# Four places for combined weights in a seven-product MoE stage, and two weight groups prepared later

## The chip, the cores and the metric

The kernel runs on one core of one Trainium2 chip. The metric is the device time of one launch in microseconds. Three runs of the kernel before gave 1232.5, 1235.75 and 1235.85 us; the median is 1235.75 us.

## What is computed

Three layers follow each other, all in float32, on 2304 tokens of width 512 (4 batches of 576).

```python
scores = scale * np.matmul(q, k.transpose(0, 1, 3, 2))     # 4 batches, 8 heads, 576 x 64
scores = np.where(mask, scores, -1000000000.0)             # causal by blocks of 64
attn = np.exp(scores - max) / (sum + 1e-09)
x = np.matmul(attn, v)                                     # to 2304 x 512
h = np.maximum(np.maximum(x @ w1, x @ w2), x @ w3)         # d_ff 768
x = h @ w_out
for e in range(4):                                         # second block, F 1024
    h = np.maximum(x @ w1[e], 0.0)
    out += p[:, e:e + 1] * (h @ w2[e])
```

## The kernel before, in words

Every float32 operand is split in a high and a low part, and each product is three matmuls (high by high, high by low, low by high) that accumulate in PSUM.

**Order of the work.** The attention goes through 16 pairs of heads (4 batches of 4). Batches 0 to 2 of the first MoE block (`moe1`, L543) run as filler work between the attention's steps: a generator yields after some matmuls, and `filler.upto` (L680) advances it to a count. While batch 2's filler work goes on, the last attention pairs run. Batch 2 ends with four output slices of `moe1_out` (L533), each with a `w_out` weight tile (`wo<-held`, 768 KB, two places).

**Fourth batch.** `moe1_last` (L573) computes the fourth batch's 512 tokens, with the 64 remaining tokens of all batches, as two halves of 384 by two halves of the width, in seven products instead of eight (Strassen-Winograd). A loop over j (3) and n (3) gives nine groups. A group has seven products `b11`, `t2`, `t1`, `b21`, `t3`, `b22`, `t4`, each of 6 matmuls 128x384 (`product`, L617). It takes three weight tiles: `w0`, of 512 KB, for b11 and b21; `w1`, of 256 KB, for t4; and `w2`, of 1 MB, which holds the combined weights of the four others. These were made earlier by `sums` (L515) and stored in DRAM as `summed`. The load of `w2` (L603) takes its place from the tags xh and xl by turns, which are the token tiles of batch 2. `w0` and `w1` take places of `wt` (three) and of the wide `wo` (two), five in turn (`WT`, L460 to 476). Between the products DVE and ACT add PSUM results and temporaries in the arena (`plus`, L589; the copy `q1`, L652; `close`, L623), the maxima stand in `mt` and `mr` (two of each), and at n = 2 the maximum is split into hh and hl (L646, L647).

**What runs beside the stage.** `combine` (L831) makes the seven token combinations (`put` with ACT's cast L803 and DVE's subtraction L804). `weights_in` (L947) prepares a first-layer weight group of the second block: a raw load of 512 KB (`t<-in_e_w`, L955), four sums on DVE (L926 to 929), two casts on ACT (L933), two subtractions on DVE (L935), a store of 1.8 MB (`ka<-w`, L958). A later call for the same group is a reload (`w<-ka`, L945). The program's tail advances the filler by counts between these calls: groups (0,2) and (0,3) first, with their store only, then (0,0) and (0,1), which stay in their places `w1`. Then comes the second block's first pass, with `hidden2` (seven products, L980) and `second` (L1062 to 1066).

**Queues and memory.** All these loads and stores are issued by SP's queue, in the order of the program. The pool `x2` (`xp`) is opened when the attention pool `attn` closes and lies on its memory; its tags are `w1` (two places of 1.8 MB), `t`, `pr` and the seven token tiles. Twelve small loads of `pr` (L784, L792) are kept in program order; `prs` and `prt` follow from them (L794 to 797). The order of the instructions on each engine is made by a scheduler from the program.

```python
for n in (2, 3):
    filler.upto(filler.done + 14)
    weights_in(0, n)
ready = []
for n in range(2):
    filler.upto(filler.done + 14)
    ready.append(weights_in(0, n))
```

Of the kernel before, what the change touches and what calls it, by code (L numbers as in the profile page):

```python
# [28 lines left out]
def program(tc, q, k, v, w123, w_out, probs, e_w1, e_w2, out):  # L29
# [64 lines left out]

    QT, QW = S - 64, S + 64
    pairs, later, made, exps, normal, least = {}, [], {}, [], [], []
    def rounded(engine, to, x):
# [445 lines left out]
    def moe1(b):  # L543
# [8 lines left out]
        for at, (ff, n) in enumerate(order):  # L552
# [3 lines left out]
            if n == 0:  # L556
                prev[ff] = mp.tile([P, MAIN], F32, name="mt", tag="mt", bufs=2)
                nc.scalar.copy(prev[ff], m)
            else:
                nc.vector.tensor_tensor(prev[ff], m, prev[ff], op=ALU.max)  # L560
# [9 lines left out]
            yield  # L570
        yield from moe1_out(b, [(MAIN, hh, hl, lambda d: x2f[b][:, d, 0:MAIN])])

    def moe1_last(xc):  # L573
# [19 lines left out]
        for j in range(NF // 2):  # L593
            state = {}
            for n in range(3):
                w0 = moe_weight(b, 6 * j + n, at)
                w1 = moe_weight(b, 6 * j + 3 + n, at + 1, KH)
                at += 2
                tag = ("xh", "xl")[n + j & 1]
                w2 = mp.tile([P, KD, MAIN], F32R, name=tag, tag=tag).rearrange(  # L600
                    "p d (s f) -> p (d s) f", s=2
                ).rearrange("p (x s) f -> p x s f", x=2)
                nc.sync.dma_start(  # L603
# [19 lines left out]
                def close(key, i, x=None):  # L623
                    if n == 0:
                        tag = ("mt", "mr")[key[1]]
                        t = mp.tile([P, (MAIN, CT)[key[1]]], F32, name=tag, tag=tag, bufs=2)[:, 0:CT]
                        state[key] = t
                        if x is None:
                            nc.scalar.copy(t, ms[i])
                        else:  # L630
                            plus(t, ms[i], x)
                    else:
                        t = state[key]
                        x = ms[i] if x is None else plus(x, ms[i], x)
                        nc.vector.tensor_tensor(t, x, t, op=ALU.max)
# [16 lines left out]
                nc.scalar.copy(q1, ms[0])  # L652
                yield
                product(1, "t2", True, False)
                u = plus(temp(), ms[1], q1)
                yield
                product(2, "t1", True, False)
                v = plus(temp(), ms[2], q1)
                yield
# [58 lines left out]
    for n in range(NALL):  # L718
# [13 lines left out]
        for m, st in enumerate(todo):  # L732
# [9 lines left out]
            at = (n + (m + 1) / len(todo)) / NPAIR  # L742
            filler.upto((at - 1) * UNITS - (LAG if b < B - 1 else 2 * LAG))
        if n + 4 < NALL:
# [85 lines left out]

    def combine(b11, b12, b21, b22):  # L831
        made = {}
# [13 lines left out]
        put("b11", b11, nc.vector)  # L846
        t1 = less(0, b12, b11)
        t2 = less(1, b22, t1)
        yield
        put("t2", t2, nc.vector)  # L850
        yield
        put("t1", t1, nc.vector)

# [421 lines left out]
    ends = [x for ds in (slice(0, KH), slice(KH, KD)) for x in (x2f[B - 1][:, ds, 0:CT], rest_x[:, ds])]  # L1275
    following = combine(*ends)
    xc = next(following)
    filler.work.append(moe1_last(xc))
    for _ in following:
        filler.upto(filler.done + 1)  # L1280
    for n in (2, 3):
        filler.upto(filler.done + 14)
        weights_in(0, n)
    ready = []
    for n in range(2):
        filler.upto(filler.done + 14)
        ready.append(weights_in(0, n))
    filler.upto(filler.done + 8)
    following = combine(*blocks(0))
    xc = next(following)  # L1290
    for _ in following:
        filler.upto(filler.done + 4)
    filler.rest()
# [32 lines left out]
    def temp():  # L1326
        return pe.tile([P, CT], F32, name="tmp", tag="tmp", bufs=NTMP)
# [149 lines left out]
```

## Time and profile before

| | |
|---|---|
| median of three runs | 1235.75 us |
| the profiled execution | 1238.21 us, its span 1236.4 us, mean granted clock 0.988 |
| PE busy | 1191.0 us (96%) |
| DVE, ACT, POOL busy | 903.2, 484.9, 282.9 us |
| DMA | 307.18 MB, mean 248 GB/s |
| the stage of the seven products | about 405 to 484 us |

Times are microseconds from the start of the span. In a timeline a row has the start, the duration, the engine, the line, the operation, output and inputs, the shape and the count; the brackets at the end tell how long the engine stood idle before it and what released it. PEclk is the granted TensorE clock, as a share of 2.4 GHz. Busy matmul times overlap in part, so the pitch of matmuls is read from rows with different counts. A DMA row gives the median from issue to landing.

### The profile page before, as it was taken

How to read it: one execution, taken by the hardware profiler on the slowest of the kernel's cores; microseconds unless marked ns; L12 is line 12 of the kernel's file. 1: busy time of each engine (PE TensorE's matmuls, PEld its weight loads, DVE VectorE, ACT ScalarE, POOL GpSimd, SP SyncE). 2: the span in 40 equal slices, each digit the busy share in tenths (PEclk: the TensorE clock that was granted, in tenths of full speed). 3: DMA queues.
4: the chain of work that ended last, by engine and by line, in shares of the span. 5: the costliest groups of instructions: out<-in, count | busy, mean ns of one | idle time of the engine just before them, and what ended most of it. 6: DMA issues, size and time to landing. Idle time of an engine off the chain costs nothing.

```text
span 1236.4 us, 18275 instructions
## 1 busy us (share of the span) xinstructions
PE 1191.0 (96%) x6887; PEld 1068.6 (86%) x6887; DVE 903.2 (73%) x1570; ACT 484.9 (39%) x1008; POOL 282.9 (23%) x300
## 2 busy tenths in 40 slices
PE   7889999999998998999999999999999999999998
PEld 4567777777776987989999998999999999999998
DVE  5867876544666676468878895768787888586896
ACT  6866664445335223234434441233232223322232
POOL 2558853442332000233343341000000000000000
PEclk8989999999999999999999999999999999999999
DMA  5836766744545894588888874867888887776754
GB/s 213 285 112 217 251 219 209 237 149 127 180 171 180 304 376 165 182 310 305 330 307 301 308 246 159 313 251 301 329 301 315 315 314 270 256 263 226 256 205 178
DMA packets 84939, 307.18 MB, mean 248 GB/s; under 512 B 9004, under 2 KB 20596, under 8 KB 69492
## 3 DMA queue, kind: packets, MB, share of 16 engines
q1 hardware_dynamic: 84852, 306.02, 68.9%
q8 instruction: 54, 0.88, 0.3%
q14 instruction: 33, 0.27, 0.1%
HBM read 213.42 MB, written 92.57 MB: 247 GB/s over the span
## 4 chain that ended last, share of the span: by engine, by line
PE 72%; DVE 10%; DMA 9%; ACT 5%; issue 2%; POOL 1%; SPq 0%; DVEq 0%; ACTq 0%; POOLq 0%
PE m L980 24%; PE o L1139 17%; PE m L487 13%; PE m L617 3%; PE tt L284 2%; PE pv L319 2%; PE st L186 2%; PE o L1062 2%; ACT p L230 2%; PE o L1066 2%; PE o L1065 2%; DMA summed<-arena 2%; PE m L1139 2%; DMA t<-in_e_w 2%; DMA part<-in_e_w 2%
## 5 line engine op out<-in xcount | busy, mean ns | idle before, releaser
L980 PE MATMUL m<-t,w 128*128 128x384 f32 x1152 | 228.4, 336 | 0.0
L1139 PE MATMUL o<-hx,w 128*128 128x384 f32 x1176 | 226.1, 337 | 0.6 <-DMA w<-kb 0.6
L1139 PEld LDWEIGHTS o<-hx,w 128*128 128x128 f32 x1176 | 207.9, 188 | 0.9 <-PE m L980 0.9
L980 PEld LDWEIGHTS m<-t,w 128*128 128x128 f32 x1152 | 203.6, 188 | 2.5
L980 PE MATMUL m<-b,w 128*128 128x384 f32 x864 | 175.5, 336 | 0.3 <-ACT tmp L1005 0.3
L980 PEld LDWEIGHTS m<-b,w 128*128 128x128 f32 x864 | 153.2, 188 | 3.7 <-ACT tmp L1005 0.7
L230 ACT ACTIVATE p<-st,mn 128x128 f32<-128x128 f32 (+2 forms) x144 | 78.6, 557 | 71.5 <-DVE mn L223 71.3
L256 POOL TENSOR_SCALAR p<-p,sm 128x128 f32<-128x128 f32 (+4 forms) x108 | 78.7, 743 | 105.7 <-ACT high L124 51.5
L1000 DVE TENSOR_TENSOR tmp<-m,tmp 128x384 f32<-128x384 f32 x144 | 78.1, 551 | 21.8 <-PE m L980 21.5
L935 POOL TENSOR_TENSOR w<-part,w 128x512 fp32r<-128x512 f32 x32 | 49.1, 1557 | 194.9 <-PE m L980 136.7
L487 PE MATMUL m<-xh,wt 128*128 128x512 f32 x256 | 85.7, 400 | 0.0
L223 DVE TENSOR_REDUCE mn<-st 128x1 f32<-128x128 f32 (+2 forms) x144 | 68.1, 512 | 16.5 <-ACT p L230 7.3
L1110 ACT CAST hx<-hq 128x768 fp32r<-128x768 f32 x49 | 40.6, 836 | 98.9 <-PE o L1139 75.8
L284 PE MATMUL tt<-ident,p 128*128 128x128 f32 x400 | 62.0, 286 | 16.1 <-ACT eh L294 6.6
L1062 PE MATMUL o<-w,hh 128*128 128x512 f32 x192 | 74.8, 391 | 0.9 <-ACT hh L1040 0.5
L1065 PE MATMUL o<-w,hh 128*128 128x512 f32 x192 | 74.9, 390 | 0.0
L1066 PE MATMUL o<-w,hl 128*128 128x512 f32 x192 | 74.8, 391 | 0.0
L284 PEld LDWEIGHTS tt<-ident,p 128*128 128x128 f32 x400 | 47.2, 145 | 30.5 <-ACT eh L294 8.3
L487 PE MATMUL m<-hh,wo 128*128 128x512 f32 x192 | 66.2, 411 | 6.6 <-DMA wo<-held 5.0
L935 POOL TENSOR_TENSOR part<-mix,part 128x512 fp32r<-128x512 f32 x32 | 44.8, 1414 | 70.0 <-ACT part L933 64.2
L1110 ACT CAST hx<-part 128x768 fp32r<-128x768 f32 x28 | 23.3, 836 | 91.4 <-PE o L1139 69.4
L1111 DVE TENSOR_TENSOR hx<-hq,hx 128x768 fp32r<-128x768 f32 x49 | 46.7, 955 | 16.0 <-ACT hx L1110 15.7
(221 smaller groups left out, 2265.0 us busy)
## 6 DMA issues: line engine op xcount, KB each, us to landing
w<-kb SPq DMA_DIRECT2D x55, 1024.0 KB, 5.5
w<-ka SPq DMA_DIRECT2D x30, 1792.0 KB, 7.8
ka<-w SPq DMA_DIRECT2D x16, 1792.0 KB, 6.7
kb<-part SPq DMA_DIRECT2D x16, 1024.0 KB, 7.0
wt<-held SPq DMA_DIRECT2D x28, 512.0 KB, 5.3
kb<-w SPq DMA_DIRECT2D x16, 768.0 KB, 4.9
arena<-in_w SPq DMA_DIRECT2D x18, 512.0 KB, 4.8
wo<-held SPq DMA_DIRECT2D x12, 768.0 KB, 5.0
```

The source lines that it names most:

```text
L223: least.append(nc.vector.tensor_reduce(mn[:, m:m + 1], x, axis=AX.X, op=ALU.min))
L230: exps.append(nc.scalar.activation(to, x, ACTF.Exp, bias=mn[:, m:m + 1], scale=-1.0, accum_out=sm[:, m:m + 1],))
L256: normal.append(nc.gpsimd.tensor_scalar(x, x, sm[:, c:c + 1], 1.0, op0=ALU.mult, op1=ALU.mult))
L284: nc.tensor.transpose(tt[:, c:c + P], pt[i][:, k0:k0 + P], ident)
L487: nc.tensor.matmul(out=out_, lhsT=w, rhs=x, start=m == 0, stop=m == n - 1)
L935: eng.tensor_tensor(w[:, a:b, 1], raw[:, a:b], f(w[:, a:b, 0]), op=ALU.subtract)
L980: ins = nc.tensor.matmul(out=m, lhsT=a, rhs=b, start=start and n == 0, stop=stop and n == 3 * KH - 1, skip_group_check=True,)
L1000: nc.vector.tensor_tensor(t, x, y, op=ALU.add)
L1062: ins = nc.tensor.matmul(out=o, lhsT=hh[:, ts], rhs=wh, start=i == 0, stop=False)
L1065: nc.tensor.matmul(out=o, lhsT=hh[:, ts], rhs=wl, start=False, stop=False)
L1066: nc.tensor.matmul(out=o, lhsT=hl[:, ts], rhs=wh, start=False, stop=i == G - 1)
L1139: nc.tensor.matmul(out=o, lhsT=a, rhs=b, start=start and m == 0, stop=stop and m == 2, skip_group_check=True,)
```

## The change

- In `moe1_last` the combined weights of the nine groups take four places in turn: xh, xl, and the two `w1` places of the second block.
- The order of products is b11, t1, t2 and so on; `combine` can put t1 first (`soon`).
- The maxima use three `mt` and one `mr`, and `mt` has three buffers.
- The second block's weight groups (0,2) and (0,3) are no longer prepared beside the stage; their first use in the first pass prepares them. Group (0,0) is prepared when eight groups have begun, (0,1) after the first pass's `combine`.
- Three attention tags, and the token tiles b11 and t1, are reserved first, which sets where they lie.
- The last batch's lag of the filler is `LAG + 0.6 * (n - 4)` instead of `2 * LAG`.

```diff
--- before.py
+++ after.py
@@ -93,6 +93,8 @@
     own = (lo, hi)
 
     QT, QW = S - 64, S + 64
+    for tag, bufs in (("raw", RAWS), ("high", 2), ("low", 2)):
+        ap_.tile([P, S + QW], F32R if bufs == 2 else F32, name=tag, tag=tag, bufs=bufs)
     pairs, later, made, exps, normal, least = {}, [], {}, [], [], []
     def rounded(engine, to, x):
         if engine is nc.scalar:
@@ -554,7 +556,7 @@
             m = ps_m.tile([P, 512], F32, name="m", tag="m")[:, 0:MAIN]
             yield from mm3(m, [(wt[:, 0, d], wt[:, 1, d], xh[:, d], xl[:, d]) for d in range(KD)])
             if n == 0:
-                prev[ff] = mp.tile([P, MAIN], F32, name="mt", tag="mt", bufs=2)
+                prev[ff] = mp.tile([P, MAIN], F32, name="mt", tag="mt", bufs=3)
                 nc.scalar.copy(prev[ff], m)
             else:
                 nc.vector.tensor_tensor(prev[ff], m, prev[ff], op=ALU.max)
@@ -570,6 +572,8 @@
             yield
         yield from moe1_out(b, [(MAIN, hh, hl, lambda d: x2f[b][:, d, 0:MAIN])])
 
+    begun = [0]
+
     def moe1_last(xc):
 
         b = B - 1
@@ -593,13 +597,17 @@
         for j in range(NF // 2):
             state = {}
             for n in range(3):
+                begun[0] += 1
                 w0 = moe_weight(b, 6 * j + n, at)
                 w1 = moe_weight(b, 6 * j + 3 + n, at + 1, KH)
                 at += 2
-                tag = ("xh", "xl")[n + j & 1]
-                w2 = mp.tile([P, KD, MAIN], F32R, name=tag, tag=tag).rearrange(
-                    "p d (s f) -> p (d s) f", s=2
-                ).rearrange("p (x s) f -> p x s f", x=2)
+                tag = ("xh", "xl", "w1", "w1")[(3 * j + n) % 4]
+                if tag == "w1":
+                    w2 = xp.tile([P, 7, 2, 2 * P], F32R, name="w1", tag="w1", bufs=2)
+                    w2 = w2.rearrange("p n x f -> p (n x) f")[:, 0:8]
+                else:
+                    w2 = mp.tile([P, KD, MAIN], F32R, name=tag, tag=tag).rearrange("p d (s f) -> p (d s) f", s=2)
+                w2 = w2.rearrange("p (x s) f -> p x s f", x=2)
                 nc.sync.dma_start(
                     out=f(w2).rearrange("p x s f -> p (x s f)"),
                     in_=summed[3 * j + n].rearrange("p x s f -> p (x s f)"),
@@ -622,8 +630,10 @@
 
                 def close(key, i, x=None):
                     if n == 0:
-                        tag = ("mt", "mr")[key[1]]
-                        t = mp.tile([P, (MAIN, CT)[key[1]]], F32, name=tag, tag=tag, bufs=2)[:, 0:CT]
+                        if len(state) < 3:
+                            t = mp.tile([P, MAIN], F32, name="mt", tag="mt", bufs=3)[:, 0:CT]
+                        else:
+                            t = mp.tile([P, CT], F32, name="mr", tag="mr")[:]
                         state[key] = t
                         if x is None:
                             nc.scalar.copy(t, ms[i])
@@ -651,11 +661,11 @@
                 q1 = temp()
                 nc.scalar.copy(q1, ms[0])
                 yield
+                product(2, "t1", True, False)
+                v = plus(temp(), ms[2], q1)
+                yield
                 product(1, "t2", True, False)
                 u = plus(temp(), ms[1], q1)
-                yield
-                product(2, "t1", True, False)
-                v = plus(temp(), ms[2], q1)
                 yield
                 product(0, "b21", False, True)
                 close((0, 0), 0)
@@ -740,7 +750,7 @@
                     weigh(n, made["pv"])
                 moe1_inputs(b, [KD - 1])
             at = (n + (m + 1) / len(todo)) / NPAIR
-            filler.upto((at - 1) * UNITS - (LAG if b < B - 1 else 2 * LAG))
+            filler.upto((at - 1) * UNITS - LAG - 0.6 * max(0, n - NPAIR))
         if n + 4 < NALL:
             load_pair(n + 4)
         if d == NPAIR - 1:
@@ -828,7 +838,7 @@
     def blocks(p):
         return [tokens(p, c, d) for d, c in ((0, 0), (0, 1), (1, 0), (1, 1))]
 
-    def combine(b11, b12, b21, b22):
+    def combine(b11, b12, b21, b22, soon=False):
         made = {}
 
         def put(name, src, low):
@@ -845,11 +855,14 @@
         yield made
         put("b11", b11, nc.vector)
         t1 = less(0, b12, b11)
+        if soon:
+            put("t1", t1, nc.vector)
         t2 = less(1, b22, t1)
         yield
         put("t2", t2, nc.vector)
         yield
-        put("t1", t1, nc.vector)
+        if not soon:
+            put("t1", t1, nc.vector)
 
         t4 = less(0, b21, t2)
         yield
@@ -1273,23 +1286,23 @@
     flat = out.rearrange("n d -> (n d)")
 
     ends = [x for ds in (slice(0, KH), slice(KH, KD)) for x in (x2f[B - 1][:, ds, 0:CT], rest_x[:, ds])]
-    following = combine(*ends)
+    for x in ("b11", "t1"):
+        xc_tile(x)
+    scratch()
+    following = combine(*ends, soon=True)
     xc = next(following)
     filler.work.append(moe1_last(xc))
     for _ in following:
         filler.upto(filler.done + 1)
-    for n in (2, 3):
-        filler.upto(filler.done + 14)
-        weights_in(0, n)
-    ready = []
-    for n in range(2):
-        filler.upto(filler.done + 14)
-        ready.append(weights_in(0, n))
+    while begun[0] < NGRP - 1:
+        filler.upto(filler.done + 1)
+    ready = [weights_in(0, 0)]
     filler.upto(filler.done + 8)
     following = combine(*blocks(0))
     xc = next(following)
     for _ in following:
-        filler.upto(filler.done + 4)
+        filler.upto(filler.done + 3)
+    ready.append(weights_in(0, 1))
     filler.rest()
     save_tails()
     moe.close()
```

**SP ahead of the stage.** `summed_107` is the last store of combined weights, `wo<-held_97` and `wo<-held_98` the `w_out` tiles of batch 2's slices 2 and 3, `pr` the twelve small loads. Before:

```order
L529 DMA summed_107<-arena 128x2048
L473 DMA wo<-held_97 128x1536
L784 DMA pr<-in_probs 128x3x4 x4
L792 DMA pr<-in_probs 128x4
L792 DMA pr<-in_probs 64x4 x2
L792 DMA pr<-in_probs 128x4 x2
L792 DMA pr<-in_probs 64x4 x2
L792 DMA pr<-in_probs 128x4
L473 DMA wo<-held_98 128x1536
L473 DMA wo<-held_81 128x2x256
```

With the change; `w_4483` and `w_4556` are the two `w1` places with the combined weights of groups 2 and 3:

```order
L531 DMA summed_107<-arena 128x2048
L475 DMA wo<-held_97 128x1536
L611 DMA w_4483<-summed_101 128x2048
L611 DMA w_4556<-summed_102 128x2048
L794 DMA pr<-in_probs 128x3x4 x4
L802 DMA pr<-in_probs 128x4
L802 DMA pr<-in_probs 64x4 x2
L802 DMA pr<-in_probs 128x4 x2
L802 DMA pr<-in_probs 64x4 x2
L802 DMA pr<-in_probs 128x4
L475 DMA wo<-held_98 128x1536
```

The loads of two groups now stand ahead of the twelve `pr` loads and of slice 3's `w_out` tile. The next rows are a piece of the same queue with what each instruction waits for, one row each (a name that begins with DMAHW is one of eight lanes, and a load waits until the transfer that had its lane before has landed):

```order
L611 DMA w_4483<-summed_101 128x2048 [waits DVE_49,PE_49,DMAHW5_49,Activation_49,Pool_49]
L611 DMA w_4556<-summed_102 128x2048 [waits DVE_49,DMAHW6_49,PE_49,Activation_49]
L794 DMA pr<-in_probs 128x3x4 [waits DMAHW7_49]
L794 DMA pr<-in_probs 128x3x4 [waits DMAHW0_49]
L794 DMA pr<-in_probs 128x3x4 [waits DMAHW1_49]
L794 DMA pr<-in_probs 128x3x4 [waits DMAHW2_49]
L802 DMA pr<-in_probs 128x4 [waits DMAHW3_49]
L802 DMA pr<-in_probs 64x4 [waits DMAHW4_49]
L802 DMA pr<-in_probs 64x4 [waits DMAHW5_49]
L802 DMA pr<-in_probs 128x4 [waits DMAHW6_49]
```

The first of the two waits for all four engines, the second for PE, DVE and ACT; the third and fourth L802 load wait for the lanes that the two have.

**DVE at the start of the stage.** `t` and `w_4380` are raw and prepared expert weights, `arena`, `mr` and `mt` temporaries and maxima of the seven products. Before:

```order
L926 TENSOR_TENSOR t<-t 128x256
L927 TENSOR_TENSOR t<-t 128x256
L929 TENSOR_TENSOR t<-t 128x256
L928 TENSOR_TENSOR t<-t 128x256
L935 TENSOR_TENSOR w_4380<-t,w_4380 128x4x256
L589 TENSOR_TENSOR arena<-m,arena 128x384
L935 TENSOR_TENSOR w_4380<-t,w_4380 128x3x256
L589 TENSOR_TENSOR arena<-m,arena 128x384 x2
L589 TENSOR_TENSOR mr<-m,arena 128x384
L589 TENSOR_TENSOR arena<-m,arena 128x384
L589 TENSOR_TENSOR mr<-m,arena 128x384
```

With the change:

```order
L939 TENSOR_TENSOR t<-t 128x256
L940 TENSOR_TENSOR t<-t 128x256
L942 TENSOR_TENSOR t<-t 128x256
L941 TENSOR_TENSOR t<-t 128x256
L593 TENSOR_TENSOR arena<-m,arena 128x384 x2
L593 TENSOR_TENSOR mt<-m,arena 128x384 x2
L593 TENSOR_TENSOR arena<-m,arena 128x384 x2
L645 TENSOR_TENSOR mt<-m,mt 128x384
L593 TENSOR_TENSOR mr<-m,arena 128x384
```

The four sums of one expert group stay there (it is now group (0,0)); the subtractions that split the weights no longer stand between the temporaries.

**PE at the start of the second block's first pass.** `m` are PSUM tiles of products, `b_` and `t_` token tiles; `w_4662`, `w_4808` before and `w_4826`, `w_5051`, `w_5370` now are the weight groups 0, 1 and 0, 1, 2. Before:

```order
L1065 MATMUL o<-w_5205,hh_5208 128x512
L1066 MATMUL o<-w_5205,hl_5209 128x512
L980 MATMUL m_5230<-t_5070,w_4662 128x384 x6
L980 MATMUL m_5318<-b_4890,w_4808 128x384 x6
L980 MATMUL m_5319<-t_4935,w_4808 128x384 x6
L980 MATMUL m_5320<-t_4973,w_4808 128x384 x6
L1062 MATMUL o<-w_5205,hh_5212 128x512
L1065 MATMUL o<-w_5205,hh_5212 128x512
L980 MATMUL m_5318<-b_5010,w_4808 128x384 x6
L1066 MATMUL o<-w_5205,hl_5213 128x512
```

With the change:

```order
L1078 MATMUL o<-w_5187,hh_5190 128x512
L1079 MATMUL o<-w_5187,hl_5191 128x512
L993 MATMUL m_5212<-t_5036,w_4826 128x384 x6
L993 MATMUL m_5300<-b_4907,w_5051 128x384 x6
L993 MATMUL m_5301<-t_4940,w_5051 128x384 x6
L993 MATMUL m_5302<-t_4972,w_5051 128x384 x6
L993 MATMUL m_5406<-b_4907,w_5370 128x384 x2
L993 MATMUL m_5407<-t_4940,w_5370 128x384 x2
L993 MATMUL m_5408<-t_4972,w_5370 128x384 x2
L1075 MATMUL o<-w_5187,hh_5194 128x512
```

Group 2's first three products now begin, two matmuls each, behind the first three of group 1; before they began later, after all of group 1.

## Rows read from the trace of the kernel before

**Rows 1.** Page, part 1: busy us (share of the span) and instructions of the engines.

```profile
PE 1191.0 (96%) x6887; PEld 1068.6 (86%) x6887; DVE 903.2 (73%) x1570; ACT 484.9 (39%) x1008; POOL 282.9 (23%) x300
```

**Rows 2.** Windows of 20 us: PE, PEld, DVE, ACT, POOL busy (instructions), PEclk, DMA share, GB/s.

```profile
420.00:440.00 20.00, 18.64 (x103) 17.36 (x102) 16.83 (x36) 6.11 (x13) 0.00 (x0) 1.00 1.03 417
440.00:460.00 20.00, 17.70 (x101) 17.06 (x100) 16.20 (x33) 7.46 (x14) 0.00 (x0) 1.00 0.97 368
...
540.00:560.00 20.00, 20.00 (x105) 18.46 (x104) 13.97 (x26) 8.51 (x15) 7.67 (x6) 1.00 0.71 264
```

**Rows 3.** Timeline of PE, 405 to 486 us: its stops (idle before, releaser).

```profile
421.49 1.32 PE L617 MATMUL m<-b,wo 128*128 128x384 f32 x6 [0.68 <-ACT arena L652]
...
423.06 2.37 PE L617 MATMUL m<-t,xh 128*128 128x384 f32 x12 [0.26 <-DMA xh<-summed]
...
426.71 1.32 PE L617 MATMUL m<-t,xh 128*128 128x384 f32 x6 [0.23 <-DVE arena L589]
...
438.62 2.35 PE L617 MATMUL m<-t,xh 128*128 128x384 f32 x12 [0.18 <-DMA xh<-summed]
...
443.43 1.32 PE L617 MATMUL m<-t,xh 128*128 128x384 f32 x6 [1.42 <-DVE arena L589]
...
459.17 1.32 PE L617 MATMUL m<-t,xh 128*128 128x384 f32 x6 [0.89 <-DVE arena L589]
...
472.08 2.35 PE L617 MATMUL m<-t,xh 128*128 128x384 f32 x12 [1.18 <-DMA xh<-summed]
```

**Rows 4.** Timeline of SP, 371 to 400 us.

```profile
371.03 0.55 SPq L603 DMA_DIRECT2D xl<-summed  x1
371.67 0.38 SPq L603 DMA_DIRECT2D xh<-summed  x1
...
380.35 2.03 SPq L784 DMA_DIRECT2D pr<-in_probs  x4
382.43 5.27 SPq L792 DMA_DIRECT2D pr<-in_probs  x8
396.37 0.33 SPq L473 DMA_DIRECT2D wo<-held  x1
```

**Rows 5.** DMA issues of 370.5 to 372.1 us: KB each, median us to landing.

```profile
xl<-summed SPq DMA_DIRECT2D x1, 1024.0 KB, 5.3
xh<-summed SPq DMA_DIRECT2D x1, 1024.0 KB, 7.1
```

**Rows 6.** Waits of SP, 376 to 412 us: total, times, longest.

```profile
SPq L792 <- DMA wo<-held: 0.9, 1, 0.9
```

**Rows 7.** Timeline of PE: last values matmuls, first matmul of output slice 3.

```profile
391.62 0.40 PE L319 MATMUL pv<-e,vraw 128*64 128x64 f32 x8
...
400.83 0.47 PE L487 MATMUL m<-hh,wo 128*128 128x512 f32 x1 [0.42 <-DMA wo<-held]
```

**Rows 8.** Timeline of PE, 486 to 503 us: the stop behind the stage.

```profile
494.73 0.79 PE L487 MATMUL m<-hh,wo 128*128 128x512 f32 x1 [4.62 <-DMA wo<-held]
...
500.44 0.48 PE L487 MATMUL m<-hl,wo 128*128 128x512 f32 x1
```

**Rows 9.** Windows of 1 us behind that stop.

```profile
495.00:496.00 1.00, 1.00 (x3) 0.81 (x4) 0.00 (x0) 0.00 (x0) 0.00 (x0) 0.50 0.90 349
```

**Rows 10.** DMA issues of 412 to 440, then of 400 to 412 us.

```profile
wt<-held SPq DMA_DIRECT2D x3, 512.0 KB, 8.7
...
wo<-held SPq DMA_DIRECT2D x1, 512.0 KB, 3.9
```

**Rows 11.** Groups of DVE by line, 405 to 484 us: busy, mean ns, idle before.

```profile
L935 DVE TENSOR_TENSOR w<-t,w 128x1024 fp32r<-128x1024 f32 (+1 forms) x8 | 8.6, 1087 | 1.6 <-ACT w L933 1.6
...
L926 DVE TENSOR_TENSOR t<-t 128x256 f32<-128x256 f32 x4 | 1.7, 420 | 5.9 <-DMA t<-in_e_w 5.9
```

**Rows 12.** Groups of ACT by line, same stretch.

```profile
L933 ACT CAST w<-t 128x1024 fp32r<-128x1024 f32 (+1 forms) x8 | 7.3, 942 | 8.1 <-DVE t L929 7.7 <-DVE t L928 0.3
```

**Rows 13.** Window of 2 us ahead of the stage.

```profile
388.00:390.00 2.00, 1.27 (x15) 0.67 (x15) 1.26 (x2) 0.86 (x2) 0.00 (x0) 1.00 0.08 9
```

## Prediction

> **What bounds the kernel now.** I read the page's busy shares first: TensorE (PE) is busy 96% of the span, 1191.0 us [rows 1]. So a change can only give back PE's idle time or its slow-clock time, and only where these lie. The windows of 20 us then show where: from 540 us on, PE has no idle at all (20.00 of 20.00), while in the stage that the change rewrites it loses 1.4 and 2.3 us per window [rows 2]. In the same windows the DMA share is 1.03 and 0.97, so the 16 DMA engines are full there.
>
> The timeline of PE from 405 us (first seven-product matmul) to 484 us names each stop [rows 3]. Four of the seven end with a temporary in the arena, which VectorE (DVE) or ScalarE (ACT) frees late: 0.68 + 0.23 + 1.42 + 0.89 = 3.22 us. Three end with a load of combined weights: 0.26 + 0.18 + 1.18 = 1.62 us. Together 4.84 us: that is all the change can win in the stage itself.
>
> After the stage stands a dearer stop: at 494.73 PE has waited 4.62 us for a `w_out` tile (`wo<-held`) [rows 8], and then runs at the lower of its two clock levels (granted clock 0.50, 1.2 GHz) until about 500.5 [rows 8, 9], instead of the 1.00 (2.4 GHz) that it has elsewhere [rows 2]. Both `wo` places are held by output slices whose last terms need the last group's maxima, and the order of the instructions there is the same in both kernels, so I leave this stop as it is.
>
> **The change part by part.** *Four places for combined weights, and two weight groups of the second block gone from the stage.* A place is now refilled some 18 to 25 us of matmuls ahead (counted in PE's order with 0.172 us per 128x384 matmul, from the rows of [rows 3]: 2.37 us for 12, 1.32 for 6, so 1.03 to 1.05 for six more). The slowest load under full DMA took 8.7 us [rows 10], so the 1.62 us go. Two of the four expert weight groups prepared there leave, with half of the 8.6 us that DVE spends on their subtractions [rows 11], their stores and their loads. The maxima temporaries come free earlier and the DMA engines are no longer full, so the 3.22 us go too. Sum: -4.8.
>
> *The w0 places.* The freed DMA time is needed: in the new PE order the shortest stretch between the last use of a 512 KB place and the first product with its next content is 30 matmuls, 5.2 us. Such a load takes 8.7 us with the DMA engines full and 3.9 us beside little traffic [rows 10]. I take the second, since two stores of 1.8 MB and two loads of 0.5 MB have left, and +0.5 for one or two that come late; ends 0 and 1.5.
>
> *Product order, third maximum buffer, reserved layout, lag.* In the PE order everything ahead of the stage is unchanged, so the lag formula moves nothing. The maxima still have four buffers. PE does the same products. Nothing, and its cover is that each is unchanged work.
>
> *The queue ahead of the stage.* This is where I expect the loss. SyncE (SP) issues all these loads in program order. Before, its row `summed` and the `wo` load of slice 2 are followed by twelve small `pr` loads and the `wo` load of slice 3. Now the two loads into the new places stand between them. Those places lie on memory of the last attention pair's probabilities, so the first load waits for PE, DVE, ACT and POOL, the second for PE's last values matmul, which starts at 391.62 and has ended at about 392.0 [rows 7]. Everything behind them on SP waits too. Before, the twelve `pr` loads were done by 387.7 (382.43 + 5.27) and the `wo` load went out at 396.37, when its place was free [rows 4].
>
> Now, step by step. The two combined loads go out at 392.0 and 392.65, spaced like the pair at 371.03 and 371.67 [rows 4]. That pair took 5.3 and 7.1 us to land [rows 5], with little else on the DMA engines, as here; so 397.3 and 399.75. The `pr` loads need a free semaphore lane: in the order with its waits, the third L802 load waits for the lane of the first combined load and the fourth for that of the second. Such a wait stands in the trace of before: a `pr` load waited 0.9 us for an earlier `wo` load to land [rows 6]. So the fourth goes out at 399.75, it and the four behind it take 5 x 0.55 us (5.27 less 0.9, over 8 [rows 4, 6]), and the `wo` load of slice 3 goes out at 402.5. It took 4.46 us to land before (396.37 to 400.83 [rows 4, 7]), so it lands at 406.95. PE wants it at 400.41, where it waited 0.42 us before [rows 7]. Idle 6.5 us instead of 0.4: **+6.1**.
>
> Ends: if no `pr` load waits for a landing, SP needs 1.1 us for the combined loads and 2.03 + 8 x 0.55 for the twelve [rows 4], and the `wo` load goes out at 399.5: +3.1. If the second combined load takes 8.7 us as under full traffic [rows 10], +7.7. What stands behind on SP and DVE (the `prs` reduction, the put of t4, the first raw load) slips as much, but it is needed only after the `wo` slice and the first products, 4.2 us and more later, so I cost it at nothing; its cover is that delay of PE itself.
>
> The Trainium skill, page "DMA: Bandwidth & Descriptors", section "Anatomy of one DMA", states that DMA engines don't wait on semaphores and that any such wait happens on the issuing sequencer before dispatch. By that rule the two combined loads hold back what follows them, which speaks against this change and gives the +6.1; if waiting loads stood in the DMA engines' rings instead, the `wo` load would go out as before and the sum would be -3.6. The trace agrees with the rule: in before SP's own row of waits charges a `pr` load with 0.9 us for a landing [rows 6].
>
> *The clock.* The stop of 4.62 us was followed by 5.7 us (494.73 to 500.44) at granted clock 0.50 [rows 8, 9]; half of that is lost: 2.85 us. Shorter stops of 0.73 us and less, as in the window 388 to 390, left it at 1.00 [rows 13]. A stop of 6.5 us is nearer the first: **+2.8**. Ends: 0, if it keeps 1.00, and 3.0.
>
> *The first pass of the second block.* The first-pass weight groups 2 and 3 are prepared there now. PE's new order starts group 2's products among group 1's. Its weights are cast after group 0's last product, with 18 matmuls (3.1 us) between, and its two casts, 0.94 us each [rows 12], fit. Group 3's raw load goes out behind group 2's store; about 15 us of products lie between that and its first use, against 8.7 us of landing [rows 10], 1.7 us of sums (4 x 0.42), one cast of 0.94 us and two subtractions of 1.09 us [rows 11, 12], 13.5 us in all. A little may show: +0.7, ends 0 and 3. Two reloads of 1.8 MB each go, but PE had no idle there [rows 2], so nothing is won.
>
> **Sum:** -4.8 + 0.5 + 6.1 + 2.8 + 0.7 = +5.3 us. It is made on the profiled execution, 1238.2 us, which stands 2.5 us above the median of the runs, 1235.75; I put the difference on the median: **1241.0 us**. The ends of the terms, if all fell together, give -1.7 and +10.4, or 1234 to 1246.
>
> **The rivals.** A measurement of this kernel can tell some 0.3%, 3.7 us, from no change: 1232.0 to 1239.5 is "the same".
>
> *The stop is short and the clock stays.* No `pr` load waits long for a landing and the stop is 3.5 us, after which PE goes on at 1.00: -4.8 + 0.5 + 3.1 + 0 + 0.7 = -0.5, so 1235.2; with half the clock loss 1236.7. For it: 3.5 us is less than 4.62, and nothing in the trace shows such a stop. Against: the lanes in the order name the two landings. 0.30.
>
> *The `wo` load is not held back (other side, faster).* If the new places are free before about 388.0 (the last pair's values reading something else there), SP has its 8.4 us (1.1 + 2.03 + 5.27) for the two loads and the twelve small ones ahead of 396.37, and the `wo` load goes out as before. Then only the stage and the first pass count: -3.6, or 1232.1, and 1231.0 if nothing new comes late. For it: SP stood idle from 387.7 to 396.37 [rows 4], so there is room. Against: the waits in the order name PE, and only the last pair's work was still to come. 0.15.
>
> *Group 3's weights late as well.* The forecast, and the first pass stops for the whole 3 us: 1243.3, and 1246 with 1.5 us more for the w0 places. Part of the slower chance, 0.10 of it.
>
> *The change does nothing there (the scheduler undoes it)* can be left out: the order of SP, DVE and PE differs in the stage.
>
> **How the numbers follow.** Forecast with late weights 0.55, short stop 0.30, not held back 0.15. By sign: slower than 1239.5 is 0.55, within 0.3% 0.30, faster than 1232.0 0.15. The range goes from 1231.5, where most of the faster case's values lie just below or at the end, to 1246.0, with about 0.1 left out at either side together with unknowns of size; the forecast's own range is 1238 to 1246.
>
> **What would show it.** In the profile of the changed kernel: SP's two combined loads near 392 and the `pr` loads after them; `wo` issued near 402.5; a PE stop of about 6.5 us near 400.4, ended by `wo<-held`, and a granted clock of 0.50 for some 5 us behind it; in the stage hardly a stop by L593 or by combined weights, and a DMA share well below 1; the stop of 4.6 us near the end of the stage still there. The prediction is wrong if the `pr` loads are done before 390 or the `wo` load goes out before 398; if the stop is there but the clock stays at 1.00, the size is wrong by 2.8; and if PE stops in the stage again on 512 KB loads, the w0 term is.

## The result, and the profile after

The changed kernel takes 1242.9 us at the median of four runs (1241.0 to 1243.9), against 1235.75 us before. The ratio is 1.0062, with a 95% interval of 1.0041 to 1.0084: slower, by more than the 0.3% that a measurement can tell, and 1.9 us above the forecast of 1241.0. A second measurement, beside the runs below, gave 1243.2 us and a ratio of 1.0051 (1.0032 to 1.0069).

The profiled execution took 1241.92 us with a span of 1240.1 us, 3.7 us more than the profiled one of before. Cut at four marks of PE's work, it differs so:

| stretch, between first matmuls of | before | after | difference |
|---|---|---|---|
| last values matmul (391.8, now 391.0) to the first seven-product matmul | 13.2 us | 21.2 us | +8.0 |
| from there to the second block's first product (510.1, now 512.5) | 105.1 us | 100.3 us | -4.8 |
| from there to the first L1139 matmul (now L1152) of the later passes (781.9, now 785.7) | 271.8 us | 273.2 us | +1.4 |
| from there to the end of the span | 454.5 us | 454.4 us | -0.1 |

(Ahead of the first mark the changed kernel is 0.8 us earlier; so the four differences make 4.5 us, and the spans differ by 3.7.) So the stage is 4.8 us shorter, and more than that is lost ahead of it. First SP's timeline after, which answers to [rows 4] (start, duration, line, output and input, count):

```profile
379.11 0.32 SPq L475 DMA_DIRECT2D wo<-held  x1
391.11 0.81 SPq L611 DMA_DIRECT2D w<-summed  x2
391.97 3.55 SPq L794 DMA_DIRECT2D pr<-in_probs  x4
395.57 5.63 SPq L802 DMA_DIRECT2D pr<-in_probs  x8
401.31 1.03 SPq L475 DMA_DIRECT2D wo<-held  x2
```

The two loads of combined weights go out at 391.11; the twelve `pr` loads come after them and not after 380, and the `w_out` load of slice 3 goes out at 401.31 instead of 396.37. SP's waits name why, and answer to [rows 6] (total, times, longest):

```profile
SPq L611 <- PE pv L321: 11.6, 1, 11.6
...
SPq L802 <- DMA w<-summed: 1.3, 1, 1.3
SPq L475 <- DMA wo<-held: 0.8, 1, 0.8
```

SP stands 11.6 us before the first of the two loads for the last values matmul. Behind it a `pr` load waits 1.3 us for a combined load to land. The 0.8 us of L475 lie behind 402.4 us, after slice 3's load has gone out, and hold back nothing ahead of it. The landings, from the DMA issues of 391 to 392 us (KB each, median us to landing):

```profile
w<-summed SPq DMA_DIRECT2D x2, 1024.0 KB, 5.9
pr<-in_probs SPq DMA_DIRECT2D x1, 6.0 KB, 7.1
```

PE's stops answer to [rows 3, 7, 8]:

```profile
405.77 0.77 PE L489 MATMUL m<-hh,wo 128*128 128x512 f32 x1 [6.20 <-DMA wo<-held]
...
473.93 0.47 PE L489 MATMUL m<-hh,wo 128*128 128x512 f32 x1 [0.77 <-DMA wo<-held]
...
497.38 0.80 PE L489 MATMUL m<-hh,wo 128*128 128x512 f32 x1 [5.13 <-DMA wo<-held]
...
542.19 2.71 PE L993 MATMUL m<-t,w 128*128 128x384 f32 x14 [1.33 <-DVE w L948]
```

The first is the forecast's: 6.20 us for slice 3's tile, 0.42 before. All seven stops of [rows 3] are gone. A new one of 0.77 us stands at the first output slice, the stop behind the stage is there with 5.13 us (4.62 before), and the first pass has one of 1.33 us for an expert weight group. The clock behind the first stop, in windows of 1 us (PE, PEld, DVE, ACT and POOL busy, then PEclk, DMA share, GB/s):

```profile
403.00:404.00 1.00, 0.00 (x0) 0.00 (x0) 0.93 (x4) 0.00 (x0) 0.00 (x0) 0.89 0.80 319
404.00:405.00 1.00, 0.00 (x0) 0.00 (x0) 0.51 (x1) 0.00 (x0) 0.00 (x0) 0.50 0.94 386
...
407.00:408.00 1.00, 1.00 (x3) 0.76 (x3) 0.00 (x0) 0.00 (x0) 0.00 (x0) 0.50 0.48 193
...
411.00:412.00 1.00, 1.00 (x6) 0.78 (x6) 0.00 (x0) 0.00 (x0) 0.00 (x0) 1.00 0.00 0
```

The granted clock falls while PE still stands and is at 1.00 again from 411 on: half clock for some 5 us of work. Slice 3's 18 matmuls took 4.2 us before (400.83 to 405.0) and take 6.4 now (405.77 to 412.2), 2.2 us more. And the stage itself, in windows of 20 us, as in [rows 2]:

```profile
420.00:440.00 20.00, 20.00 (x117) 20.00 (x116) 12.40 (x26) 3.17 (x8) 0.00 (x0) 1.00 0.77 249
440.00:460.00 20.00, 20.00 (x116) 19.81 (x115) 13.93 (x29) 3.96 (x10) 0.00 (x0) 1.00 0.72 224
540.00:560.00 20.00, 18.67 (x92) 16.26 (x92) 18.61 (x33) 8.54 (x15) 6.96 (x5) 1.00 0.89 328
```

PE is full in the stage (18.64 and 17.70 before), with a DMA share of 0.77 and 0.72 instead of 1.03 and 0.97. The window from 540 us, full before, holds the 1.33 us.

### The profile page after: what moved, and what is told of

Its sections match the earlier page's. It is cut to its first block, busy times and chain, and to the rows that moved or that the text cites. A ratio compares the mean times of both kernels' runs of the same rounds, so it can differ in the third digit from the quotient of the medians.

```text
span 1240.1 us, 18286 instructions
## 1 busy us (share of the span) xinstructions
PE 1191.9 (96%) x6887; PEld 1069.8 (86%) x6887; DVE 903.8 (73%) x1570; ACT 486.0 (39%) x1008; POOL 283.4 (23%) x300
## 4 chain that ended last, share of the span: by engine, by line
PE 66%; DVE 14%; DMA 11%; ACT 5%; issue 2%; POOL 1%; SPq 0%; DVEq 0%; ACTq 0%; POOLq 0%
PE m L993 20%; PE o L1152 17%; PE m L489 13%; PE m L625 5%; DMA t<-in_e_w 4%; PE tt L286 2%; PE pv L321 2%; PE st L188 2%; DMA summed<-arena 2%; ACT p L232 2%; PE m L1152 2%; DVE w L948 2%; DVE hl L1054 2%; DMA part<-in_e_w 1%; DVE tmp L1013 1%
## 5 line engine op out<-in xcount | busy, mean ns | idle before, releaser
L1152 PE MATMUL o<-hx,w 128*128 128x384 f32 x1176 | 226.1, 337 | 0.5 <-DMA w<-kb 0.5
L1152 PEld LDWEIGHTS o<-hx,w 128*128 128x128 f32 x1176 | 207.9, 188 | 0.8 <-PE m L993 0.8
L489 PEld LDWEIGHTS m<-hh,wo 128*128 128x128 f32 x192 | 38.0, 200 | 24.1 <-issue 6.8
```

The source lines that it names most:

```text
L489: nc.tensor.matmul(out=out_, lhsT=w, rhs=x, start=m == 0, stop=m == n - 1)
L1152: nc.tensor.matmul(out=o, lhsT=a, rhs=b, start=start and m == 0, stop=stop and m == 2, skip_group_check=True,)
```

## The experiments

All times are medians; each ratio is to the kernel before on the same chip, which had 1235.8 us in the first four runs and 1236.8 in the last four.

**The two loads behind the `pr` loads.**

```diff
-                nc.sync.dma_start(
+                ins = nc.sync.dma_start(
...
+                if 3 * j + n in (2, 3):
+                    tc.keep_in_program_order(ins)
```

> The change with one thing different: the loads of combined weights for groups 2 and 3 (into the w1 places) are pinned behind the stage's own weight loads on SP, so that the twelve pr loads and the w_out load of slice 3 no longer stand behind them. Theory A (the loss is SP's queue): the slice-3 w_out load goes out near 396, the PE stop near 400 falls from 6.2 us to under 1 us, the clock stays at 1.00 behind it, and the time falls by 5.8 + 2.2 = 8 us, to about 1235. Rival B (the stop is slack that the stage gets back later, through DMA and DVE that have caught up meanwhile): the stop goes, new stops come in the stage, and the time falls by less than 4 us. Rival C (the loss is in the first pass and the layout): no change, 1241 to 1244.

Measured: 1233.4 us, ratio 0.9978 (0.9966 to 0.9989). That is 9.5 us below the changed kernel, where 8 was told, and faster than the kernel before. SP and PE:

```profile
381.64 5.27 SPq L804 DMA_DIRECT2D pr<-in_probs  x8
395.57 4.64 SPq L475 DMA_DIRECT2D wo<-held  x2
```

```profile
399.94 0.47 PE L489 MATMUL m<-hh,wo 128*128 128x512 f32 x1 [0.32 <-DMA wo<-held]
...
465.59 0.47 PE L489 MATMUL m<-hh,wo 128*128 128x512 f32 x1 [0.76 <-DMA wo<-held]
...
488.72 0.65 PE L489 MATMUL m<-hh,wo 128*128 128x512 f32 x1 [5.11 <-DMA wo<-held]
```

The `pr` loads end at 386.9, the `w_out` load goes out at 395.57, the stop is 0.32 us, and the clock stays at 1.00 from 400 to 420. Theory A holds; B and C fall, since no new stop of any size came in the stage (only the 0.76 us that the changed kernel has too). The change without this queue is a gain of about 2.7 us. One more us of the difference can be placed: behind the stop of 5.11 us the clock was 0.50 for 3.4 us of work in this execution (488.9 to 492.3), and for 5.4 us in that of the changed kernel (497.4 to 502.8).

**Two places instead of four.**

```diff
-                tag = ("xh", "xl", "w1", "w1")[(3 * j + n) % 4]
+                tag = ("xh", "xl")[n + j & 1]
```

> The change with the combined weights in two places (xh, xl) as before; the two weight groups still go to the first pass, and the products, maxima and layout are the change's. Theory A: no load waits for the attention's memory, so the stop near 400 falls to under 1 us and the time to about 1235, as in the run with the pinned loads; the freed DMA time makes the two places enough, with at most 1 us of stops on combined weights. Rival B (four places carry the gain of the stage): stops on combined weights of 2 us or more, time 1237 or above.

Measured: 1236.1 us, ratio 0.9996 (0.9982 to 1.0010).

```profile
400.38 0.47 PE L489 MATMUL m<-hh,wo 128*128 128x512 f32 x1 [0.65 <-ACT arena L542]
...
421.08 2.37 PE L625 MATMUL m<-t,xh 128*128 128x384 f32 x12 [0.72 <-DMA xh<-summed]
...
489.86 0.79 PE L489 MATMUL m<-hh,wo 128*128 128x512 f32 x1 [5.77 <-DMA wo<-held]
```

The stop near 400 is gone, as A says, and one stop on combined weights is left, 0.72 us. The time is 2.7 us above the pinned run, and no better than before (0.9996): with two places nothing is left of the gain over the kernel before. In the stage itself six of the seven stops are gone with two places too, so there most comes from the weight groups that left. Of the 2.7 us the profiles show 0.72 at this stop, 0.33 at the stop near 400 (0.65 against 0.32), 0.66 behind the stage (5.77 against 5.11), and about 1.2 by the clock there: 0.50 for 5.8 us of work, against 3.4 in the pinned run. That the last of these hangs on the places, and not on the single execution, is not shown.

**The `pr` loads much earlier, the two loads left where they are.**

```diff
+    pr = const.tile([P, NTT, E], F32, name="pr")
...
+        if n == 10:
+            load_probs()
```

> The change with the twelve pr loads issued much earlier (at the eleventh attention pair, into a tile of the constant pool); the two loads of combined weights still wait on SP for the last values matmul ahead of slice 3's w_out load. Theory A, as I told it: the loss needs both, the wait and the twelve small loads behind it with their lanes. With the small loads gone the w_out load can go out at about 392 to 393, and in fact when its place is free, near 396, so the stop near 400 is under 1 us and the time about 1235. Rival (the wait of the two loads alone holds the w_out load, or their 2 MB slow it on the DMA engines): a stop of 2 to 6 us stays and the time is 1238 to 1243.

Measured: 1237.4 us, ratio 1.0013 (1.0003 to 1.0024). SP, then PE:

```profile
391.81 0.81 SPq L612 DMA_DIRECT2D w<-summed  x2
396.23 4.61 SPq L476 DMA_DIRECT2D wo<-held  x2
```

```profile
401.42 0.47 PE L490 MATMUL m<-hh,wo 128*128 128x512 f32 x1 [1.14 <-DMA wo<-held]
```

The two loads still wait until 391.81, and yet the `w_out` load goes out at 396.23, when its place is free. It takes 5.1 us to land, 4.2 in the pinned run, and the stop is 1.14 us: a little more than I had told. So the wait alone does not hold the `w_out` load; it takes the wait and the twelve loads that stand behind it. The time came out 2.4 us higher than told, 4 us above the pinned run. In the profiles the extra over the pinned run lies in the stop near 400 (0.8 us), in the stop behind the stage (5.97 against 5.11 us) with its slow clock, and ahead of the stage (0.7 us). There the twelve loads do in small what they did near 400: they now go out from 272.8 to 279.5, the `wo` load behind them goes out at 279.57 and not at 273.21 as in the pinned run, and PE has a stop of 0.91 us at 283.93 that no other run has, with the clock at 0.50 until 287. So this run tells what the wait does without the small loads, but its time is not a clean price of the wait.

**The pinned loads, and slice 2's tile of the fourth batch in the xl place.**

```diff
-        wt = weight_tile(n, wide)
+        if b == B - 1 and n == 3 * NF + 2:
+            wt = mp.tile([P, KD, MAIN], F32R, name="xl", tag="xl").rearrange("p d f -> p (d f)")[:, 0:2 * NF * P]
+            wt = wt.rearrange("p (k a f) -> p k a f", k=2, a=NF)
+        else:
+            wt = weight_tile(n, wide)
```

> As the run with the pinned loads, and the fourth batch's w_out tile of slice 2 is put into the xl place (free after group 5) instead of a wo place. Theory: the stop of 5.1 us behind the stage (both wo places held until the last group's terms) goes, and with it the half-clock stretch of about 5 us behind it (2.5 us): 7.6 us less than the pinned run, about 1227.5. Rival 1: the stop moves to slice 3, whose wo place is freed late too: gain under 4 us. Rival 2: the clock falls all the same, since ACT, DVE and the token products stop PE elsewhere: gain 5 us.

Measured: 1225.6 us, ratio 0.9914 (0.9895 to 0.9934): 7.8 us below the pinned run, the fastest of all the runs.

```profile
400.13 0.47 PE L493 MATMUL m<-hh,wo 128*128 128x512 f32 x1 [0.49 <-DMA wo<-held]
...
490.88 0.47 PE L493 MATMUL m<-hh,wo 128*128 128x512 f32 x1 [0.79 <-DMA wo<-held]
...
504.90 1.34 PE L999 MATMUL m<-t,w 128*128 128x384 f32 x6 [0.87 <-DVE tmp L1019]
```

The stop behind the stage is 0.79 us instead of 5.11, and the clock stays at 1.00 in every window of 5 us from 485 to 540. Both rivals fall: nothing moved to slice 3, and the clock did not fall. That 7.6 was told and 7.8 came is in part luck: the profiled executions differ by 6.1 us (spans of 1230.0 and 1223.9), 4.3 of stop and 1.7 of clock, since in the pinned run's profile the half clock lasted 3.4 us and not the 5 that the working took.

**The changed kernel again, and four of the twelve `pr` loads early.**

> The changed kernel itself once more, beside the next runs on one chip. Its four runs gave 1242.9 us against 1235.8 us before, while its profiled execution was only 3.7 us above the profiled one of before. If the four runs are typical: 1241 to 1244. If the profiled pair is: 1239 to 1240.

Measured: 1243.2 us (1239.9 to 1245.4), ratio 1.0051; its profiled execution took 1245.3 us, with a stop of 6.58 us at the same place. So the four runs are typical.

Then the same edit as in the run with the early `pr` loads, with the four loads of the first two passes in `load_probs` and the eight of the tails (L802) left where they are:

```diff
+    pr = const.tile([P, NTT, E], F32, name="pr")
...
+    def load_probs():
+        for p in range(NPASS - 1):
+            for c in range(2):
...
+        if n == 10:
+            load_probs()
```

> The change with four of the twelve pr loads issued early; the two loads of combined weights and eight pr loads stand ahead of slice 3's w_out load. By the lanes in its order, the last two of the eight now wait for the landing of the two combined loads (5.9 us each in the changed kernel, from 391.1 and 391.6), so the w_out load goes out at about 398.5 and the PE stop is about 3.3 us instead of 6.2. What is open is the clock. Theory (a stop lowers the clock only if it is long): 3.3 us is too short, the granted clock stays at 1.00 and the time is 2.9 + 2.2 = 5 us below the changed kernel. Rival (any stop of some us costs a stretch at half clock, as one of 1.8 us near 200 us did): 0.50 for 3 us or more behind it, and the time is only 3 us below the changed kernel.

Measured: 1242.6 us (1236.2 to 1244.1), ratio 1.0035 (1.0021 to 1.0050). SP's waits, the stop, the clock, and a row ahead of them:

```profile
SPq L805 <- DMA w<-summed: 2.8, 2, 2.2
```

```profile
405.43 0.47 PE L490 MATMUL m<-hh,wo 128*128 128x512 f32 x1 [4.01 <-DMA wo<-held]
```

```profile
404.00:405.00 1.00, 0.00 (x0) 0.00 (x0) 0.14 (x1) 0.00 (x0) 0.00 (x0) 1.00 0.97 371
...
407.00:408.00 1.00, 1.00 (x4) 0.71 (x3) 0.00 (x0) 0.00 (x0) 0.00 (x0) 0.50 0.11 45
408.00:409.00 1.00, 1.00 (x4) 0.80 (x3) 0.86 (x3) 0.00 (x0) 0.00 (x0) 0.50 0.00 0
...
410.00:411.00 1.00, 1.00 (x6) 0.80 (x6) 0.00 (x0) 0.00 (x0) 0.00 (x0) 1.00 0.00 0
```

```profile
386.08 3.46 PE L287 MATMUL tt<-ident,p 128*128 128x128 f32 x15 [0.73 <-POOL p L259]
```

The two lane waits are there, 2.8 us together, and the stop is 4.01 us, not 3.3. Through all of it the clock is still 1.00; it falls to 0.50 when PE is already at work again, and is back at 410. My theory of the clock falls by these rows: in this execution a stop of 4 us costs a stretch of half clock too, only later. The time decides less. By the ratios the run is 2 us below the changed kernel on that chip, nearer the rival's 3 than 5, by the medians 0.6, and the two intervals overlap; its runs spread over 8 us. The profiled execution also ran at 0.50 from 386.5 to 389.7, ahead of the two loads: the 15 matmuls of the last row take 3.46 us, 1.86 in the changed kernel, so 1.6 us of its time are lost before the stop.

**The parts costed at nothing, put back.**

```diff
-                product(2, "t1", True, False)
-                v = plus(temp(), ms[2], q1)
-                yield
                 product(1, "t2", True, False)
                 u = plus(temp(), ms[1], q1)
                 yield
+                product(2, "t1", True, False)
+                v = plus(temp(), ms[2], q1)
+                yield
```

and the maxima in two `mt` and two `mr`, two `mt` buffers, and the old lag and combinations.

> As the run with the pinned loads, with the parts that I costed at nothing put back as they were before: the order of products b11, t2, t1, the combinations in the old order, two mt and two mr for the maxima, mt with two buffers, and the old lag. Theory: nothing hangs on them now that the weights have left the stage, so 1233.4 as the pinned run, within 1.5 us. Rival (they carry the gain of the stage): stops on the arena's temporaries come back, up to 3.2 us, and the time is 1235 to 1237.

Measured: 1234.8 us, ratio 0.9977 (0.9960 to 0.9995), the same as the pinned run.

```profile
400.41 0.47 PE L489 MATMUL m<-hh,wo 128*128 128x512 f32 x1 [0.33 <-DMA wo<-held]
...
490.70 0.80 PE L489 MATMUL m<-hh,wo 128*128 128x512 f32 x1 [7.68 <-DMA wo<-held]
```

No stop on a temporary came back. The 0.76 us at the first output slice is gone here, and the stop behind the stage is 7.68 us instead of 5.11. How these two hang on the order of the products wasn't tried apart.

**The kernel before, with slice 2's tile in the xl place.** The edit is that of the run with the tile in the xl place, without the pinned loads.

> The kernel before with one thing different: the fourth batch's w_out tile of slice 2 is put into the xl place, which group 7 leaves one group before the end. Theory: the stop of 4.6 us behind the stage and the half-clock stretch behind it (2.85 us) go, as they did in the changed kernel with pinned loads: 7.5 us less than before, about 1228. Rival: with the DMA engines full there, the load of 768 KB into xl (8 us) comes late or delays others, and the gain is under 4 us.

Measured: 1229.1 us, ratio 0.9936 (0.9920 to 0.9951): 7.7 us below before. Its windows of 5 us behind the stage:

```profile
485.00:490.00 5.00, 5.00 (x29) 4.36 (x28) 1.65 (x5) 1.38 (x4) 0.00 (x0) 1.00 0.44 144
490.00:495.00 5.00, 5.00 (x33) 4.49 (x32) 0.16 (x1) 1.03 (x2) 0.00 (x0) 1.00 0.89 260
495.00:500.00 5.00, 5.00 (x27) 4.28 (x27) 0.00 (x0) 0.96 (x2) 0.00 (x0) 1.00 0.62 199
```

PE is full and at 1.00, where before it was busy for 0.38 of the 5 us from 490 and had a clock of 0.50 from 495. The stop behind the stage, which the change left as it was, was worth more than the whole stage.

## Why the prediction was right, and where its sizes were off

The forecast was slower at 1241.0 us, and the mechanism was the one told: SP's queue. Step by step, from the profiles:

- *The stage, -4.8.* All seven stops went, as told. But the term is too small for that: a stop costs more than the idle time of its row (below). By the runs the pinned kernel gains 2.7 us, since the other small terms stand against this one.
- *The w0 places, +0.5.* One stop of 0.77 us, at the load whose stretch had been counted as short (the first output slice's tile goes out at 467.93, into the place that the eighth group's `w0` leaves, with 30 matmuls between).
- *The queue, +6.1.* 6.20 less 0.42 is 5.8 us. Two parts of the working were off against each other. The first four `pr` loads took 3.55 us behind the two large ones, not 2.03, and the waits for a lane came to 1.3 us, where the prediction's steps hold 3.0 (1.1 and 1.9). In all the `w_out` load went out 10.2 us after the first combined load, where the prediction had 10.5; that the two errors cancel is luck. The pinned run shows that this order makes the stop, and the run with the `pr` loads early shows that it takes both.
- *The clock, +2.8.* 2.2 us by slice 3's matmuls. The rival "the stop is short and the clock stays" had the stop wrong, and its view of the clock falls with the 4.01 us stop, behind which the clock did fall. It need not have waited for a run: that "nothing in the trace shows such a stop" is a misreading, since the kernel before has one of 1.84 us near 202.5 with half clock behind it (rows at the end).
- *The first pass, +0.7.* One stop of 1.33 us for an expert weight group, DVE's subtraction last, as told, for group 3, inside the ends of 0 and 3; from its raw load (524.40) to the end of that subtraction (542.13) it took 17.7 us, where the prediction counted 13.5; the two small stops of before there (0.34 and 0.55 us) are gone.
- *Product order, maxima and lag, nothing.* Right within the measurement: 0.9977 and 0.9978 without and with. The stop behind the stage did move by 2.6 us, so it is the sum that is nothing, and not each part.

Term by term these give -4.8 + 0.8 + 5.8 + 2.2 + 1.3 - 0.9 and 0.5 for the longer stop behind the stage: +4.9 us, against +4.5 in the profiles from the last values matmul on. That they agree is partly luck. For the stage the terms give -3.5 and the stretch shrank by 4.8; for the stretch behind it they give +0.4 and it grew by 1.4. The first of these comes from what a stop costs, as four rows of the kernel before show:

```profile
425.27 1.21 PE L617 MATMUL m<-b,wt 128*128 128x384 f32 x6
426.71 1.32 PE L617 MATMUL m<-t,xh 128*128 128x384 f32 x6 [0.23 <-DVE arena L589]
427.87 1.20 PE L617 MATMUL m<-b,xh 128*128 128x384 f32 x6
428.91 1.20 PE L617 MATMUL m<-b,wt 128*128 128x384 f32 x6
```

Without a stop the products start 1.04 us apart (427.87 to 428.91); around the stop of 0.23 us they start 1.44 and 1.16 us apart, 0.52 us more in all. Some 0.29 us on top of the row for each of the seven stops that went, less the one that came, is an estimate of 1.7 us from these rows; "all the change can win in the stage" was more than 4.84 us. In the stretch behind, one stop was overlooked: at 750.85 PE waits 1.52 us for a temporary that ACT frees (1.75 us in the second profile of the changed kernel), 0.33 us before at 746.91. So PE was not without idle after 540 us before either, since [rows 2] show only 540 to 560. The pinned run has no such stop there; what makes it was not tried.

The runs say +6 to +7 us. The two profiled executions of the changed kernel differ by 3.4 us (1241.9 and 1245.3), and 2.0 of these lie ahead of the last values matmul. The clock differs there: near 70 us it was at 0.50 for about 10 us in the second execution and in that of the kernel before, and for about 3.4 us in the first (mean granted clock from 62 to 90 us: 0.82, 0.82 and 0.94). Against the second, the span of before is 7.1 us shorter (1236.4 and 1243.5), as much as the runs say. That the first pair differs by only 3.7 us is thus in part the luck of one execution.

One sum of the prediction does not come out: the rival with late weights has 1243.3 us, and 1.5 us more make 1244.8, not 1246. Nothing else is built on it.

On the rule of the Trainium skill, page "DMA: Bandwidth & Descriptors", section "Anatomy of one DMA" (a DMA's semaphore wait happens on the issuing sequencer before dispatch; the section is on loads that GpSimd issues, these are SP's): the trace agrees. SP's own rows carry the 11.6 us, and pinning two loads took the stop away.

## What to carry to other kernels

Giving a load a place that comes free late is a cost to everything that stands behind it on its queue: look for the waiting load's position in the queue's order, count the dispatch of what follows (twelve loads of a few KB took SP 9.2 us here), and ask which of these the bottleneck engine wants first. The small loads alone, ahead of the stop (pinned run), left a stop of 0.32 us, the wait alone 1.14 us; together they made 6.20 us and cost 8 us with the clock. Moving the small loads elsewhere is no cure by itself: at 272.8 they held back another tile. And before work goes into a stage with 4.8 us of stops in seven places, the one stop beside it that also drops the clock is worth a look: one tile in another place gave 7.7 us.

## What the runs showed that I had not expected

- A stop can cost clock after it is over: through the stop of 4.01 us the granted clock was 1.00, and it was 0.50 only when PE had gone on; with the stop of 6.20 us it fell within the stop, at about 403.8. The trace of the kernel before had this already, with a stop of 1.84 us that ended at 202.55 (PE's row, then a window of 2 us; the clock fell at about 203.6):

```profile
202.55 0.50 PE L487 MATMUL m<-xh,wu 128*128 128x512 f32 x1 [1.84 <-ACT mt L558]
204.00:206.00 2.00, 2.00 (x6) 1.59 (x5) 1.60 (x1) 0.20 (x1) 2.00 (x2) 0.50 0.23 37
```

- The length of a stop alone does not tell what happens to the clock: the same stop, 1.85 us at 202.10 in the run with the parts put back, left it at 1.00, and so did the 1.33 us at 542.19; behind 0.91 us at 283.93 in the run with the early `pr` loads it was 0.50.
- Four `pr` loads of 6 KB took SP 3.55 us behind two loads of 1 MB (3.46 in the second profile), and 2.03 before; the one issued with the large loads took 7.1 us to land. The eight of 1 to 2 KB did not take longer: 4.2 us without their waits behind the same two loads in the run with four early, against 4.4 before. Why the four do is not shown.
